# Feed-forward tiles of 512 tokens with matmuls of 512 columns, two output banks, and x @ w_in sharing its banks with y

## The chip, the cores and the metric

The kernel runs on one core of one Trainium2 chip. The metric is the device time of one launch in microseconds, as a median over several timed runs. A core has a matrix engine (TensorE; PE in the profile, with its weight loads listed apart as PEld), VectorE (DVE), ScalarE (ACT), GpSimd (POOL) and SyncE (SP), which issues the DMAs. Matmul results go to PSUM; in this kernel all of its eight banks (2 KB per partition, 512 fp32 columns) are handed out to named pools.

## The reference, cut to what matters

A chunked state-space scan over 4 batches, 8 heads and 768 positions makes a vector of 256 for each of 3072 tokens; a feed-forward layer with the nonlinearity h - tanh(h) follows.

```python
# x (4, 8, 768, 32), a (4, 8, 768), B and C (4, 8, 768, 16)
for c in range(nc):                       # chunks of the sequence
    cum = np.cumsum(la, axis=-1)          # la = log a of the chunk
    M = einsum('bhin,bhjn->bhij', Cc, Bc) * exp(cum_i - cum_j) * causal
    y[chunk] = M @ xc + (Cc @ state) * exp(cum)
    state = decay_full * state + sum_j(Bc_j xc_j * decay_from_j)
x = y.transpose(0, 2, 1, 3).reshape(3072, 256)
h = x @ w_in                              # (256, 2048)
out = (h - np.tanh(h)) @ w_out            # (2048, 256)
```

## The kernel before, in words

**Scan.** Each batch is cut into 7 chunks, six of Q = 112 positions and one of 96, 28 chunks in all. The 16 rows ahead of a chunk's positions hold the state, so that one matmul gives both the part within the chunk and the part from the state. For a chunk, `chunk_a` (lines 424 to 470) makes `att` on PE (lines 437 and 443), ACT takes the exponential (447), DVE multiplies (451), POOL masks (454), and the result `lt` is the moving operand of `chunk_y` (472 to 529): its matmuls (488) write `y` to a PSUM bank, eight heads times 112 positions, and those of line 496 write the new state beside it. ACT copies the state in four pieces into the next chunk's operand (`fn_c`, 501), ACT rounds y to `xh` (508), and DVE takes the rest as `xl` (513). `y` has one bank. From chunk 9 on the `att` of the next chunk is issued with the `y` of this one. Chunks 0 to 2 go through `first_tile`, which does not use `rt_c`. `rt_c` and `lt_c` hold the cumulative sums of the decays as bf16 parts; they come back from DRAM by DMAs in `get_parts` (780 to 785), and before that DVE fills `rt_c` (415).

**Feed-forward.** The 3072 tokens are 12 tiles of TT = 256, and the 2048 hidden columns are 8 pairs u of two blocks of 128. A step is one tile t and one pair u. `mm1` (532 to 551) makes `ph` = x @ w_in for the pair: two blocks times six matmuls of 256 columns (high by high, high by low, low by high, each over two halves of the 256 features), into one of the two banks of pool `ph`. `act` (553 to 582): ACT tanh (561), DVE h - tanh (565), ACT rounding to `gh` (569), DVE rest `gl` (576). `mm2` (584 to 613), LAG = 2 steps later in the written order, adds the pair to both halves of the output with twelve matmuls of 256 columns (602). Both halves e = 0, 1 stand side by side in the one bank of pool `po`. At the last tile the second half goes to a part of the `att` banks instead (named `end`). The result is copied to `ob` (640 to 644) and stored (647).

**Order.** Tiles 0 to 3 go through four passes of two pairs each, since the weights arrive and are split while they run (`conv`, 272 to 319, on ACT and DVE); their partial outputs are kept in `pt` (618, 625). Tiles 4 to 11 take all 8 pairs in one go. Chunks are planned into the steps of the tile ahead of the one that needs them. All operations are first recorded in `Order` (lines 48 to 187) with an engine, an estimated cost, and what they read and write. A buffer is a slot of a named ring; slots of a ring are taken in the order of recording, and a slot can be taken when the readers of its last user are done. `Order` then tries 16 list schedules and issues the instructions in the order of the shortest. Each engine runs its instructions in that order.

Of the kernel before, what the change touches and what calls it, by code (L numbers as in the profile page):

```python
# [30 lines left out]
TT = 256  # L31
NT = T // TT
# [158 lines left out]
def tile_ssm_moe(ctx: ExitStack, tc: tile.TileContext, a, x, bn, bc, wts, out):  # L191
# [9 lines left out]
    ps_y = ctx.enter_context(tc.tile_pool(name="ps_y", bufs=1, space=PSUM))  # L201
# [155 lines left out]
    def first_tile():  # L357
# [39 lines left out]
        for ck in range(len(chunks[0])):  # L397
# [74 lines left out]
    def chunk_y(ck):  # L472
# [31 lines left out]
        def fn_h():  # L504
            if c == 0:
                seq[b]["xh"] = p3.tile([P, 2, S], F32R, tag="xh", name=f"xh{b}", bufs=2)
            k["yv"] = k["y"][:, 0 : 2 * Q].rearrange("p (g q) -> p g q", g=2)[:, :, 0:q]
            nc.scalar.copy(seq[b]["xh"][:, :, c * Q : c * Q + q], k["yv"])

        def fn_l():  # L510
            if c == 0:
                seq[b]["xl"] = p3.tile([P, 2, S], F32R, tag="xl", name=f"xl{b}", bufs=2)
            nc.vector.tensor_tensor(out=seq[b]["xl"][:, :, c * Q : c * Q + q], in0=k["yv"],  # L513
                                    in1=seq[b]["xh"][:, :, c * Q : c * Q + q].bitcast(F32), op=ALU.subtract)
# [17 lines left out]
    def mm1(t, u):  # L532
        b, j = divmod(t, S // TT)
        d, ts = seq[b], slice(j * TT, (j + 1) * TT)
        cs = [c for c in range(CPB) if c * Q < ts.stop and (c + 1) * Q > ts.start]
        n_h, n_g = slot("ph", NPH), slot("g", 3)
        gs[t, u, 0] = [n_h, n_g]

        def fn():
            ph = ps_h.tile([P, 2, TT], F32, tag="ph", name=f"ph{t}_{u}")  # L540
            gs[t, u] = [ph]
            for j in range(2):

                for p in range(2):
                    for k in range(2):
                        for w_ in (wh, wl)[: 2 - p]:
                            nc.tensor.matmul(out=ph[:, j, :], lhsT=w_[:, u, 0, k, j * P : (j + 1) * P],  # L547
                                             rhs=d[("xh", "xl")[p]][:, k, ts], start=p == 0 and k == 0 and w_ is wh,
                                             stop=p == 1 and k == 1, skip_group_check=True)

        op("PE", 1.41, fn, r=[*[d["n_xh"][c] for c in cs], *[d["n_xl"][c] for c in cs], f"wh{u}.0", f"wl{u}.0"], w=[n_h])

    def act(t, u, eng):
        n_h, n_g = gs[t, u, 0]
        n_gh, n_gl = slot("gh", 3), slot("gl", 3)
        gs[t, u, 0] += [n_gh, n_gl]

        def fn_t():
            g = p3.tile([P, 2, TT], F32, tag="g", name=f"g{t}_{u}")
            gs[t, u].append(g)  # L560
            nc.scalar.activation(g, gs[t, u][0], AF.Tanh)  # L561

        def fn_s():
            ph, g = gs[t, u]
            nc.vector.tensor_tensor(out=g, in0=ph, in1=g, op=ALU.subtract)  # L565

        def fn_h():
            gh = p3.tile([P, 2, TT], F32R, tag="gh", name=f"gh{t}_{u}")
            nc.scalar.copy(gh, gs[t, u][1])  # L569
            gs[t, u].append(gh)  # L570

        def fn_l():
            _, g, gh = gs[t, u]
            gl = p3.tile([P, 2, TT], F32R, tag="gl", name=f"gl{t}_{u}")
            on = nc.vector if eng == "DVE" else nc.gpsimd
            on.tensor_tensor(out=gl, in0=g, in1=gh.bitcast(F32), op=ALU.subtract)  # L576
            gs[t, u].append(gl)
# [4 lines left out]
        op(eng, 0.8 if eng == "DVE" else 1.8, fn_l, r=[n_g, n_gh], w=[n_gl])  # L582

    def mm2(t, u, seg):

        _, _, n_h, n_l = gs[t, u, 0]
        if u == seg[0]:
            n_po[t, seg] = slot("po", 1)

        def fn():  # L590
            _, _, gh, gl = gs[t, u]
            if u == seg[0]:
                po[t, seg] = [ps_o.tile([P, 2, TT], F32, tag="po", name=f"o{t}_{u}")] * 2
                if end:

                    po[t, seg][1] = ps_a.tile([P, 2, TT], F32, tag="att", name="end")

            for es in ((0,), (1,)) if end and u == seg[-1] else ((0, 1),):
                for k, (w_, g) in enumerate(((wh, gh), (wl, gh), (wh, gl))):
                    for j in range(2):  # L600
                        for e in es:
                            nc.tensor.matmul(out=po[t, seg][e][:, e, :], lhsT=w_[:, u, 1, j, e * P : (e + 1) * P],  # L602
                                             rhs=g[:, j, :], start=u == seg[0] and k == 0 and j == 0 and (e == 0 or end),
                                             stop=u == seg[-1] and k == 2 and j == 1, skip_group_check=True)
# [10 lines left out]
    def keep(t, seg):  # L615

        if seg[0]:
            op("DVE", 0.69, lambda: nc.vector.tensor_tensor(out=pts[t], in0=po[t, seg][0], in1=pts[t], op=ALU.add),
               r=[n_po[t, seg]], w=[n_pt[t]])
            return  # L620
        n_pt[t] = slot("pt", NSW)

        def fn():
            pts[t] = p1.tile([P, 2, TT], F32, tag="pt", name=f"pt{t}", bufs=NSW)
            nc.scalar.copy(pts[t], po[t, seg][0])

        op("ACT", 0.6, fn, r=[n_po[t, seg]], w=[n_pt[t]])

    def store(t, seg):
        name = op.pieces(slot("ob", 2), 2)  # L630

        def fn_c(i):
            if i == 0:
                obs[t] = p2.tile([P, 2, TT], F32, tag="ob", name=f"ob{t}")
                if t == NT - 1:

                    obs["end"] = p2.tile([P, 2, TT], F32, tag="ob", name="ob_end")
            ob1 = obs["end" if t == NT - 1 else t][:, 1]
            if t in pts:
                nc.vector.tensor_tensor(out=obs[t], in0=po[t, seg][0], in1=pts[t], op=ALU.add)  # L640
            elif i == 0:
                nc.scalar.copy(obs[t][:, 0], po[t, seg][0][:, 0])
            else:
                nc.vector.tensor_copy(out=ob1, in_=po[t, seg][1][:, 1])

        def fn_d(i):
            nc.sync.dma_start(out=out[i * P : (i + 1) * P, t * TT : (t + 1) * TT], in_=obs["end" if t == NT - 1 and i else t][:, i])

        if t < NSW:
            op("DVE", 0.69, lambda: fn_c(0), r=[n_po[t, seg], n_pt[t]], w=name)  # L650
        else:
            op("ACT", 0.36, lambda: fn_c(0), r=[n_po[t, seg]], w=[name[0]])
            op("DVE", 0.36, lambda: fn_c(1), r=[n_po[t, seg]], w=[name[1]])
        for i in range(2):
            op("SP", 0.42, lambda i=i: fn_d(i), r=[name[i]], dma=KB)
# [23 lines left out]
    rt_c = cp.tile([P, 2, NCK, P], BF16, name="rt_c")  # L679
# [100 lines left out]
    def get_parts(i, k, sl):  # L780
        src = cum3[i // 2].rearrange("p (e w c) m -> p e w c m", e=2, w=2)[:, i % 2, :, sl].rearrange("p w c m -> p w (c m)")
        if k == 0:
            nc.sync.dma_start(out=lt_c[32 * i + 3 : 32 * i + 9, sl], in_=src)
        else:
            nc.sync.dma_start(out=rt_c[32 * i : 32 * i + 3, :, sl].rearrange("p w c m -> p w (c m)"), in_=src)

    n_pr = slot("y", 1)
# [7 lines left out]
    n_pq2 = slot("po", 1)  # L795
# [98 lines left out]
```

## Time and profile before

| what | value |
|---|---|
| timed runs | 345.36, 346.02, 348.71 us |
| median | 346.02 us |
| span of the profiled execution, first to last instruction | 342.5 us |
| median less that span | 3.5 us |
| busy: PE, PEld, DVE, ACT, POOL | 328.7, 318.0, 226.9, 193.3, 54.2 us |
| matmuls of 256 columns | 2304, at lines 547 and 602 |
| mean granted TensorE clock | 0.980 of full |

The profiled execution has no time of its own in the records beside its span; where a time is compared, the median stands for it. The page of the profile gives busy time and share per engine, 40 slices of the span as tenths of busy time with the granted clock, the chain of work that ended last followed back from the end, and groups of equal instructions with what they waited for. The trace can also be asked for the instructions in order of time, for busy times in chosen windows, and for all uses of one tile. A busy PE is not PE at its peak: matmuls overlap, so distances between starts are read instead of durations.

### The profile page before, as it was taken

Reading aid. Unit: us, or ns where it says so; the run is one execution under the profiler, and the core shown is the slowest. Engines: PE = TensorE matmul, PEld = TensorE weight load, DVE = VectorE, ACT = ScalarE, POOL = GpSimd, SP = SyncE. Lnnn points to the kernel's source line nnn. Section 1 sums busy time; section 2 is a strip of 40 time slices with the busy share of each in tenths; the row PEclk is TensorE's granted clock in tenths of the full one; section 3 lists DMA queues with packets and bytes.
Section 4 is the critical chain, followed back from the end, with each engine's and each line's share of the span. In section 5 each row is a group of like instructions: output and inputs, shape, how many; then the busy total and the mean of one; then the engine's idle time right before and its main releaser. Section 6 shows DMA issues by size and latency. Waiting matters only on the chain.

```text
span 342.5 us, 8855 instructions
## 1 busy us (share of the span) xinstructions
PE 328.7 (96%) x3756; PEld 318.0 (93%) x3756; DVE 226.9 (66%) x339; ACT 193.3 (56%) x403; POOL 54.2 (16%) x69
## 2 busy tenths in 40 slices
PE   9759879999999999999999999999999999999996
PEld 7648769999999999999999999999999999999996
DVE  5898999989899656744655654654655654654552
ACT  8866788857453445734745644634645654534441
POOL 1536444101000101210211210210211110100000
PEclk9956999999999999999999999999999999999999
DMA  5939693910000012300301210210200000000000
GB/s 173 272 90 286 165 297 103 257 45 15 16 2 0 2 59 80 92 15 2 91 15 31 63 31 2 63 29 2 63 3 1 33 2 2 31 2 2 31 2 32
DMA packets 12471, 21.39 MB, mean 62 GB/s; under 512 B 2848, under 2 KB 7648, under 8 KB 12432
## 3 DMA queue, kind: packets, MB, share of 16 engines
q1 hardware_dynamic: 12432, 20.84, 21.0%
q8 instruction: 29, 0.48, 0.6%
q14 instruction: 10, 0.08, 0.1%
HBM read 17.51 MB, written 3.32 MB: 61 GB/s over the span
## 4 chain that ended last, share of the span: by engine, by line
PE 91%; DVE 5%; ACT 1%; POOL 1%; issue 1%; POOLq 0%; DVEq 0%; ACTq 0%
PE ph L547 40%; PE o L602 38%; PE y L488 4%; PE att L443 3%; PE end L602 2%; PE att L437 1%; PE warm L729 1%; DVE lt L389 1%; DVE wm L295 1%; PE y L496 1%; DVE lt L451 1%; DVE rt_c L415 1%; PE cp L366 1%; DVE wv L299 1%; POOL lt L394 0%
## 5 line engine op out<-in xcount | busy, mean ns | idle before, releaser
L561 ACT ACTIVATE g<-ph 128x512 f32<-128x512 f32 x96 | 57.4, 598 | 82.3 <-PE ph L547 78.5
L565 DVE TENSOR_TENSOR g<-ph,g 128x512 f32<-128x512 f32 x96 | 66.1, 689 | 55.4 <-ACT g L561 54.5
L547 PE MATMUL ph<-xh,wh 128*128 128x256 f32 x384 | 101.4, 286 | 0.0
L547 PE MATMUL ph<-xh,wl 128*128 128x256 f32 x384 | 100.2, 282 | 0.0
L576 DVE TENSOR_TENSOR gl<-g,gh 128x512 fp32r<-128x512 f32 x96 | 67.9, 708 | 28.7 <-ACT gh L569 27.4
L569 ACT CAST gh<-g 128x512 fp32r<-128x512 f32 x96 | 59.3, 619 | 34.0 <-DVE g L565 32.9
L547 PE MATMUL ph<-xl,wh 128*128 128x256 f32 x384 | 77.0, 282 | 0.0
L547 PEld LDWEIGHTS ph<-xh,wh 128*128 128x128 f32 x384 | 73.2, 191 | 1.4 <-issue 0.4
L547 PEld LDWEIGHTS ph<-xh,wl 128*128 128x128 f32 x384 | 73.1, 190 | 0.0
L602 PE MATMUL o<-gh,wh 128*128 128x256 f32 x368 | 61.2, 284 | 0.0
L602 PE MATMUL o<-gh,wl 128*128 128x256 f32 x368 | 59.6, 279 | 0.0
L602 PE MATMUL o<-gl,wh 128*128 128x256 f32 x368 | 59.6, 279 | 0.0
L547 PEld LDWEIGHTS ph<-xl,wh 128*128 128x128 f32 x384 | 59.6, 190 | 0.0
L454 POOL TENSOR_SCALAR_AFFINE_SELECT lt<-lt 128x896 f32<-128x896 f32 (+1 forms) x25 | 28.2, 1128 | 155.5 <-DVE lt L451 150.9
L602 PEld LDWEIGHTS o<-gh,wh 128*128 128x128 f32 x368 | 50.5, 188 | 1.5
L602 PEld LDWEIGHTS o<-gl,wh 128*128 128x128 f32 x368 | 50.6, 188 | 0.0
L602 PEld LDWEIGHTS o<-gh,wl 128*128 128x128 f32 x368 | 50.5, 187 | 0.0
L451 DVE TENSOR_TENSOR lt<-att,lt 128x896 f32<-128x896 f32 (+1 forms) x25 | 26.7, 1067 | 11.3 <-ACT lt L447 11.1
L447 ACT ACTIVATE lt<-att 128x896 f32<-128x896 f32 (+1 forms) x25 | 22.6, 905 | 11.2 <-PE att L443 10.7
L501 ACT COPY x<-y 16x64 f32<-16x64 f32 x96 | 19.5, 203 | 7.6 <-DVE xl L513 6.9
L488 PE MATMUL y<-lt,x 128*32 128x112 f32 (+1 forms) x448 | 17.1, 272 | 7.0 <-POOL bc L337 3.0
L330 POOL TENSOR_TENSOR bw<-braw,wdec 128x256 f32<-128x256 f32 x14 | 13.2, 945 | 52.1 <-PE y L496 47.7
(77 smaller groups left out, 249.9 us busy)
## 6 DMA issues: line engine op xcount, KB each, us to landing
raw<-w_d SPq DMA_DIRECT2D x16, 512.0 KB
x<-x_d SPq DMA_DIRECT2D x14, 256.0 KB
bc<-bc_d SPq DMA_DIRECT2D x56, 60.0 KB
out_d<-ob SPq DMA_DIRECT2D x23, 128.0 KB
braw<-bn_d SPq DMA_DIRECT2D x14, 112.0 KB
cum<-parts SPq DMA_DIRECT2D x1, 168.0 KB
out_d<-ob_end SPq DMA_DIRECT2D x1, 128.0 KB
lt_c<-cum SPq DMA_DIRECT2D x4, 27.0 KB
```

The costliest lines, as they stand in the source:

```text
L330: nc.gpsimd.tensor_tensor(out=d["b"].rearrange("p c (h n) -> p c h n", h=H), in0=d["braw"].rearrange("p c (h n) -> p c h n", h=H), in1=wd. ...
L447: nc.scalar.activation(k["l"][:, :, 0:q].rearrange("p (i w) q -> p i w q", i=4), k["a"][:, :, 0:2, :], AF.Exp)
L451: nc.vector.tensor_tensor(out=lt, in0=k["a"][:, :, 2:4, :], in1=lt, op=ALU.mult)
L454: nc.gpsimd.affine_select(out=k["l"][:, :, 0:q], in_=k["l"][:, :, 0:q], pattern=[[0, H], [1, q]], compare_op=ALU.is_ge, fill=0.0, base=N, ...
L488: nc.tensor.matmul(out=y[D * h : D * h + D, hg * Q : hg * Q + q], lhsT=d["x"][:, cg, P * hg + D * h : P * hg + D * h + D], rhs=k["l"][:, 4 ...
L501: nc.scalar.copy(grp[(ck + 1) // CPG]["x"][0:N, (ck + 1) % CPG, 2 * D * i : 2 * D * i + 2 * D], k["y"][D * i : D * i + N, H * D : H * D + ...
L547: nc.tensor.matmul(out=ph[:, j, :], lhsT=w_[:, u, 0, k, j * P : (j + 1) * P], rhs=d[("xh", "xl")[p]][:, k, ts], start=p == 0 and k == 0 an ...
L561: nc.scalar.activation(g, gs[t, u][0], AF.Tanh)
L565: nc.vector.tensor_tensor(out=g, in0=ph, in1=g, op=ALU.subtract)
L569: nc.scalar.copy(gh, gs[t, u][1])
L576: on.tensor_tensor(out=gl, in0=g, in1=gh.bitcast(F32), op=ALU.subtract)
L602: nc.tensor.matmul(out=po[t, seg][e][:, e, :], lhsT=w_[:, u, 1, j, e * P : (e + 1) * P], rhs=g[:, j, :], start=u == seg[0] and k == 0 and ...
```

## The change

- Tiles 0 to 3 keep 256 tokens; tokens 1024 to 3071 are four tiles of 512 (`WIDTH`). A step of a wide tile is one block of 128 hidden columns in place of a pair: six matmuls of 512 columns in `mm1`, six in `mm2`. `ph`, `g`, `gh` and `gl` keep their size of 128x512.
- The output has two banks, `po0` and `po1`, one for each half. `mm2` goes through all matmuls of half 0 and then through those of half 1. Keeping and storing is done half by half, on 128x256 for narrow and 128x512 for wide tiles. The special case of the last tile is gone.
- Pool `y` is gone. The `y` of chunks 0 to 2 and the sums at the start use `po0` and `po1`; from chunk 3 on `y` takes a slot of the ring `ph`, which stays at two banks.
- `xh` and `xl` are one ring of 1536 positions in place of two buffers of 768, so that the tile of tokens 2048 to 2559 can lie across two batches.
- `rt_c` is 112 wide in place of 128; its loads become two DMAs in place of one, eight more in all. `parts` moves to the buffers of `ob`.
- Planner costs: 1.31 for a wide block of matmuls beside 1.41 for a narrow pair.

```diff
-TT = 256
-NT = T // TT
+WIDTH = 256, 256, 256, 256, 512, 512, 512, 512
+NT = len(WIDTH)
+START = [sum(WIDTH[:t]) for t in range(NT + 1)]
+BANK = 512
+RING = 2 * S
...
-    ps_y = ctx.enter_context(tc.tile_pool(name="ps_y", bufs=1, space=PSUM))
...
     def chunk_y(ck):
-        n_y = slot("y", 1)
+        at0 = b % 2 * S + c * Q
+        tag = f"po{1 - ck % 2}" if ck < len(chunks[0]) else "ph"
+        n_y = slot(tag, NPH if tag == "ph" else 1)
...
-            y = k["y"] = ps_y.tile([P, 2 * H * D], F32, tag="y", name=f"y{ck}")
+            y = k["y"] = (ps_h if tag == "ph" else ps_o).tile([P, BANK], F32, tag=tag, name=f"y{ck}")
...
-            nc.scalar.copy(seq[b]["xh"][:, :, c * Q : c * Q + q], k["yv"])
+            nc.scalar.copy(xh[:, :, at0 : at0 + q], k["yv"])
...
-    def mm1(t, u):
+    def blocks(t):
+        return BANK // WIDTH[t]
+
+    def mm1(t, f):
+        w = WIDTH[t]
+        ts = slice(START[t] % RING, START[t] % RING + w)
...
-            for j in range(2):
+            for i in range(blocks(t)):
+                u, j = divmod(f + i, 2)
                 for p in range(2):
                     for k in range(2):
                         for w_ in (wh, wl)[: 2 - p]:
-                            nc.tensor.matmul(out=ph[:, j, :], lhsT=w_[:, u, 0, k, j * P : (j + 1) * P],
-                                             rhs=d[("xh", "xl")[p]][:, k, ts], ...
+                            nc.tensor.matmul(out=ph[:, i * w : i * w + w], lhsT=w_[:, u, 0, k, j * P : (j + 1) * P],
+                                             rhs=(xh, xl)[p][:, k, ts], ...
-        op("PE", 1.41, fn, ...
+        op("PE", 1.41 if w == 256 else 1.31, fn, ...
...
     def mm2
-            n_po[t, seg] = slot("po", 1)
+            n_po[t, seg] = [slot(f"po{e}", 1) for e in range(2)]
...
-            for es in ((0,), (1,)) if end and u == seg[-1] else ((0, 1),):
+            for e in range(2):
                 for k, (w_, g) in enumerate(((wh, gh), (wl, gh), (wh, gl))):
-                    for j in range(2):
-                        for e in es:
-                            nc.tensor.matmul(out=po[t, seg][e][:, e, :], lhsT=w_[:, u, 1, j, e * P : (e + 1) * P],
-                                             rhs=g[:, j, :], ...
+                    for i in range(blocks(t)):
+                        u, j = divmod(f + i, 2)
+                        nc.tensor.matmul(out=po[t, seg][e][:, 0:w], lhsT=w_[:, u, 1, j, e * P : (e + 1) * P],
+                                         rhs=g[:, i * w : i * w + w], ...
...
     def store(t, seg):
+        for e in range(2):
+            old = [n_pt[t][e]] if t < NSW else []
+            op("DVE" if t < NSW or e else "ACT", cost, lambda e=e: fn_c(e), r=[n_po[t, seg][e], *old], w=[name[e]])
+            op("SP", 0.42, lambda e=e: fn_d(e), r=[name[e]], dma=KB * w // 256)
...
-    rt_c = cp.tile([P, 2, NCK, P], BF16, name="rt_c")
+    rt_c = cp.tile([P, 2, NCK, Q], BF16, name="rt_c")
...
     def get_parts(i, k, sl):
-            nc.sync.dma_start(out=rt_c[32 * i : 32 * i + 3, :, sl].rearrange("p w c m -> p w (c m)"), in_=src)
+            for w in range(2):
+                nc.sync.dma_start(out=rt_c[32 * i : 32 * i + 3, w, sl], in_=src[:, w, :, N:P])
...
-    segs = [(t, tuple(range(i, j))) for i, j in zip(SWEEPS, SWEEPS[1:]) for t in range(NSW)]
-    segs += [(t, tuple(range(NCONV))) for t in range(NSW, NT)]
+    segs = [(t, (2 * i, 2 * j)) for i, j in zip(SWEEPS, SWEEPS[1:]) for t in range(NSW)]
+    segs += [(t, (0, NF)) for t in range(NSW, NT)]
+    steps = [(t, f, seg) for t, seg in segs for f in range(*seg, blocks(t))]
```

More of the change, by code (lines that the diff above doesn't have):

```diff
@@ L210, in tile_ssm_moe @@
     for t in range(NT):
-        b, j = divmod(t, S // TT)
-        end = b * CPB + -(-(j + 1) * TT // Q)
+        b, r = divmod(START[t + 1] - 1, S)
+        end = b * CPB + r // Q + 1
         chunks[t], ends = list(range(ends, end)), end
@@ L436, in fn_p @@
                 r = slice(32 * i, 32 * i + 9)
-                nc.tensor.matmul(out=at_[:, i, 0:2, :], lhsT=lt_c[r, ck], rhs=rt_c[r, :, ck, N : N + q],
+                nc.tensor.matmul(out=at_[:, i, 0:2, :], lhsT=lt_c[r, ck], rhs=rt_c[r, :, ck, 0:q],
                                  start=True, stop=True)
@@ L529, in chunk_y @@
         op("DVE", 0.4, fn_l, r=[n_y, n_xh], w=[n_xl])
-    def mm1(t, u):
-        b, j = divmod(t, S // TT)
-        d, ts = seq[b], slice(j * TT, (j + 1) * TT)
-        cs = [c for c in range(CPB) if c * Q < ts.stop and (c + 1) * Q > ts.start]
+    def blocks(t):
[3 more added lines that the diff above has]
+        ts = slice(START[t] % RING, START[t] % RING + w)
+        n = [x for b in seq for c in range(CPB) if b * S + c * Q < START[t] + w
+             and b * S + min((c + 1) * Q, S) > START[t] for x in (seq[b][0][c], seq[b][1][c])]
         n_h, n_g = slot("ph", NPH), slot("g", 3)
-        gs[t, u, 0] = [n_h, n_g]
+        gs[t, f, 0] = [n_h, n_g]
         def fn():
-            ph = ps_h.tile([P, 2, TT], F32, tag="ph", name=f"ph{t}_{u}")
-            gs[t, u] = [ph]
-            for j in range(2):
+            ph = ps_h.tile([P, BANK], F32, tag="ph", name=f"ph{t}_{f}")
+            gs[t, f] = [ph]
+            for i in range(blocks(t)):
+                u, j = divmod(f + i, 2)
                 for p in range(2):
@@ L546, in fn @@
                         for w_ in (wh, wl)[: 2 - p]:
[L547 to L548 removed]
+                            nc.tensor.matmul(out=ph[:, i * w : i * w + w], lhsT=w_[:, u, 0, k, j * P : (j + 1) * P],
+                                             rhs=(xh, xl)[p][:, k, ts], start=p == 0 and k == 0 and w_ is wh,
@@ L569, in fn_h @@
-            nc.scalar.copy(gh, gs[t, u][1])
-            gs[t, u].append(gh)
+            gh = p3.tile([P, BANK], F32R, tag="gh", name=f"gh{t}_{f}")
+            nc.scalar.copy(gh, gs[t, f][1])
+            gs[t, f].append(gh)
         def fn_l():
[L573 to L577, printed above, removed]
+            _, g, gh = gs[t, f]
@@ L579, in act @@
+            gl = p3.tile([P, BANK], F32R, tag="gl", name=f"gl{t}_{f}")
+            nc.vector.tensor_tensor(out=gl, in0=g, in1=gh.bitcast(F32), op=ALU.subtract)
+            gs[t, f].append(gl)
         op("ACT", 0.6, fn_t, r=[n_h], w=[n_g])
@@ new lines, in act, with mm2 @@
+        op("DVE", 0.71, fn_l, r=[n_g, n_gh], w=[n_gl])
+    def mm2(t, f, seg):
+        w, last = WIDTH[t], f + blocks(t) == seg[1]
+        _, _, n_h, n_l = gs[t, f, 0]
+        if f == seg[0]:
+            n_po[t, seg] = [slot(f"po{e}", 1) for e in range(2)]
+        def fn():
+            _, _, gh, gl = gs[t, f]
+            if f == seg[0]:
+                po[t, seg] = [ps_o.tile([P, BANK], F32, tag=f"po{e}", name=f"o{t}_{f}_{e}") for e in range(2)]
+            for e in range(2):
+                for k, (w_, g) in enumerate(((wh, gh), (wl, gh), (wh, gl))):
+                    for i in range(blocks(t)):
+                        u, j = divmod(f + i, 2)
+                        nc.tensor.matmul(out=po[t, seg][e][:, 0:w], lhsT=w_[:, u, 1, j, e * P : (e + 1) * P],
+                                         rhs=g[:, i * w : i * w + w], start=f == seg[0] and k == 0 and i == 0,
+                                         stop=last and k == 2 and i == blocks(t) - 1, skip_group_check=True)
+        op("PE", 1.41 if w == 256 else 1.31, fn, r=[n_h, n_l, f"wh{f // 2}.1", f"wl{f // 2}.1"], w=n_po[t, seg])
+        if last:
+            if seg[1] < NF:
@@ L615, in keep @@
     def keep(t, seg):
[L617 to L627, printed above, removed]
+        w = WIDTH[t]
+        cost = 0.36 if w == 256 else 0.6
@@ new lines, in keep, with fn @@
+        if seg[0] == 0:
+            n_pt[t] = op.pieces(slot(f"pt{t}", 1), 2)
+        def fn(e):
+            o = po[t, seg][e][:, 0:w]
+            if seg[0]:
+                nc.vector.tensor_tensor(out=pts[t][:, e], in0=o, in1=pts[t][:, e], op=ALU.add)
+                return
+            if e == 0:
+                pts[t] = p1.tile([P, 2, w], F32, tag=f"pt{t}", name=f"pt{t}")
+            nc.scalar.copy(pts[t][:, e], o)
+        for e in range(2):
+            op("DVE" if seg[0] else "ACT", cost, lambda e=e: fn(e), r=[n_po[t, seg][e]], w=[n_pt[t][e]])
@@ L629, in store, with fn_c @@
     def store(t, seg):
+        w = WIDTH[t]
+        cost = 0.36 if w == 256 else 0.6
         name = op.pieces(slot("ob", 2), 2)
[L632 to L638, printed above, removed]
+        def fn_c(e):
+            if e == 0:
+                obs[t] = p2.tile([P, 2, w], F32, tag="ob", name=f"ob{t}")
+            o, out_ = po[t, seg][e][:, 0:w], obs[t][:, e]
@@ L639, in fn_c @@
             if t in pts:
-                nc.vector.tensor_tensor(out=obs[t], in0=po[t, seg][0], in1=pts[t], op=ALU.add)
-            elif i == 0:
-                nc.scalar.copy(obs[t][:, 0], po[t, seg][0][:, 0])
-            else:
[L644 to L653, printed above, removed]
@@ L654, in store, with fn_d @@
-        for i in range(2):
-            op("SP", 0.42, lambda i=i: fn_d(i), r=[name[i]], dma=KB)
+                nc.vector.tensor_tensor(out=out_, in0=o, in1=pts[t][:, e], op=ALU.add)
+            elif e == 0:
+                nc.scalar.copy(out_, o)
+            else:
+                nc.vector.tensor_copy(out=out_, in_=o)
+        def fn_d(e):
+            nc.sync.dma_start(out=out[e * P : (e + 1) * P, START[t] : START[t] + w], in_=obs[t][:, e])
+        for e in range(2):
+            old = [n_pt[t][e]] if t < NSW else []
+            op("DVE" if t < NSW or e else "ACT", cost, lambda e=e: fn_c(e), r=[n_po[t, seg][e], *old], w=[name[e]])
+            op("SP", 0.42, lambda e=e: fn_d(e), r=[name[e]], dma=KB * w // 256)
@@ L672, in tile_ssm_moe @@
     wdec = cp.tile([P, H, NCK], F32, name="wdec")
-    rows = p2.tile([P, 2, TT], F32, tag="ob", name="rows")[:, 0].rearrange("p (i q) -> p i q", i=2)
-    rest = p2.tile([P, 2, TT], F32, tag="ob", name="rest")[:, 0].rearrange("p (i q) -> p i q", i=2)
-    parts = cp.tile([P, 2, 3, P], BF16, name="parts")
+    both = p2.tile([P, 2, 2, P], F32, tag="ob", name="both")
+    rows, rest = both[:, 0], both[:, 1]
+    xh = cp.tile([P, 2, RING], F32R, name="xh")
+    xl = cp.tile([P, 2, RING], F32R, name="xl")
+    parts = p2.tile([P, 2, 3, P], BF16, tag="ob", name="parts")
     lt_c = cp.tile([P, NCK, P], BF16, name="lt_c")
-    rt_c = cp.tile([P, 2, NCK, P], BF16, name="rt_c")
+    rt_c = cp.tile([P, 2, NCK, Q], BF16, name="rt_c")
     cum3 = dr.tile([2, 3, 4 * NCK, P], BF16, name="cum3")
@@ L753, in sums_rows @@
     def sums_rows():
-        pr = misc["pr"] = ps_y.tile([P, 4, P], F32, tag="y", name="pr")
+        pr = misc["pr"] = ps_o.tile([P, 4, P], F32, tag="po1", name="pr")
         misc["pq"] = pr.rearrange("p i q -> p (i q)")[:, 2 * P :]
@@ L838, in tile_ssm_moe @@
         if g < len(steps):
-            t, u, _ = steps[g]
-            mm1(t, u)
-            act(t, u, "DVE")
+            t, f, _ = steps[g]
+            mm1(t, f)
+            act(t, f)
             for fn, args in todo.get(g, ()):
```

62 lines of the change are left out of this document (20 added, 42 removed).

## The prediction

> **What bounds the kernel now.** I read the page first: shares, slices, chain.
>
> ```profile
> span 342.5 us, 8855 instructions
> PE 328.7 (96%) x3756; PEld 318.0 (93%) x3756; DVE 226.9 (66%) x339; ACT 193.3 (56%) x403; POOL 54.2 (16%) x69
> PE   9759879999999999999999999999999999999996
> PEclk9956999999999999999999999999999999999999
> PE 91%; DVE 5%; ACT 1%; POOL 1%; issue 1%; POOLq 0%; DVEq 0%; ACTq 0%
> ```
>
> PE is the chain, and PE is full from the eighth slice on. Then the busy times by stage:
>
> ```profile
> 20.00:40.00 20.00, 16.38 (x248) 14.84 (x252) 18.16 (x24) 12.74 (x30) 9.10 (x10) 0.69 0.73 210
> 40.00:60.00 20.00, 18.08 (x308) 16.80 (x309) 19.51 (x26) 16.58 (x40) 9.09 (x9) 1.00 0.66 189
> 60.00:80.00 20.00, 20.00 (x172) 20.00 (x171) 18.68 (x25) 13.78 (x22) 2.23 (x3) 1.00 0.44 128
> ...
> 160.00:180.00 20.00, 20.00 (x262) 19.28 (x265) 12.02 (x17) 11.24 (x26) 2.85 (x4) 1.00 0.16 46
> ...
> 300.00:320.00 20.00, 20.00 (x172) 20.00 (x172) 9.70 (x16) 8.25 (x16) 0.00 (x0) 1.00 0.01 1
> ```
>
> The columns are the stretch, its length, PE, PEld, DVE, ACT and POOL busy (with counts), the granted clock, DMA share, GB/s. Before 60 us DVE is nearly full and PE has gaps; from 60 us PE has none, with DVE and ACT near half load after 160. So there the time is the number of matmuls times the distance between their starts (the pitch). That pitch and what moves it:
>
> ```profile
> 192.57 2.83 PE ph L547 x24
> ...
> 24.00:27.00 3.00, 3.00 (x16) 2.71 (x13) 3.00 (x5) 2.26 (x4) 1.12 (x1) 0.50 0.65 161
> 24.45 0.41 PE L547 MATMUL ph<-xh,wl 128*128 128x256 f32 x1
> 26.37 0.63 PE L547 MATMUL ph<-xl,wh 128*128 128x256 f32 x2
> ...
> 5.27 0.54 PE L763 MATMUL pr<-la,upto 128*128 128x224 f32 x2
> 5.65 1.94 PE L366 MATMUL cp<-upto,la 128*128 128x112 f32 x16
> 7.51 0.71 PE L377 MATMUL att<-bc 16*128 16x112 f32 x16
> 5.27:5.65 0.38, 0.38 (x5) 0.38 (x4) 0.00 (x0) 0.37 (x3) 0.24 (x1) 1.00 0.91 334
> 5.65:7.51 1.86, 1.86 (x17) 1.75 (x16) 1.56 (x5) 1.86 (x2) 0.00 (x0) 1.00 1.06 371
> ```
>
> The chain's row gives 2.83 / 24 = 117.9 ns for 256 columns at full clock. At clock 0.50 nine matmuls lie between 24.45 and 26.37: 213.3 ns, so 106.7 for the columns alone at full clock. Some 11 ns are thus not columns. What they are, the start of the kernel tells, at clock 1.00: sixteen cp matmuls of 112 columns take 5.65 to 7.51, 116.3 ns each; two pr matmuls of twice the columns, also fp32 with 128x128 weights, take 190 ns each. If fp32 costs two cycles a column, 224 columns are 186.7 ns and 112 are 93.3. The long one pays 3.3 ns over its columns, the short one is held at 116. So about 117 ns looks like a floor for one matmul that brings 128x128 weights, whatever its columns, and above it little is added.
>
> **The change part by part.** *512 columns.* Of 2304 feed-forward matmuls (the rows L547 and L602 of the page: 3 x 384, 3 x 368, and 3 x 16 into "end") tiles 4 to 11 hold 1536; they become 768 of 512 columns, with half the weight loads. Pitch of a new one: at least 213.3 (columns alone); at most 235.8 (two old ones, nothing gained); 224.5 if 11.2 ns go with every matmul. I take 213.3 + 3.3 = 216.6, by the pr row, the nearest stream longer than the floor. Gain 768 x (235.8 - 216.6) = **14.7 us** (17.3 at 213.3; 8.7 at 224.5; 0).
>
> The Trainium skill, "TensorE: Matmul & The Clock Gate", section "Back-to-back issue gap", gives the isolated gap as N/2.4 + 2.5 ns. For 512 that is 215.8 and the gain would be 15.4 us; for 256 it gives 109.2, where the trace has 117.9. The same page's section on LDWEIGHTS has 128 columns loading in 106.7 ns: the floor read above is 10 ns over it.
>
> *y takes a bank of ph.* I call m(g) the twelve (or six) matmuls that make step g's ph, and m2 those that take its g to the output. From chunk 3 on y is one more user of the two ph banks, in the written order m, y, m. The block m(g+1) behind y needs the bank of m(g), and m(g+2) needs y's.
>
> ```profile
> 312.32 0.63 PE L602 MATMUL o<-gh,wh 128*128 128x256 f32 x4
> 312.58 0.60 ACT L561 ACTIVATE g<-ph 128x512 f32<-128x512 f32 x1 [0.85 <-PE ph L547]
> 313.21 0.69 DVE L565 TENSOR_TENSOR g<-ph,g 128x512 f32<-128x512 f32 x1 [0.76 <-ACT g L561]
> ...
> 161.09 0.59 PE L488 MATMUL y<-lt,x 128*32 128x112 f32 x16
> 162.38 0.39 PE L547 MATMUL ph<-xh,wh 128*128 128x256 f32 x1
> 163.40 0.34 ACT L508 CAST xh<-y 128x224 fp32r<-128x224 f32 x1
> 165.01 0.39 DVE L513 TENSOR_TENSOR xl<-y,xh 128x224 fp32r<-128x224 f32 x1 [0.38 <-ACT x L501]
> 165.44 0.42 ACT L501 COPY x<-y 16x64 f32<-16x64 f32 x2 [0.46 <-DVE xl L513]
> ```
>
> An m frees its bank 313.90 - 312.32 = 1.6 us after PE leaves it. Between two m with a y between lie an m2 (6 x 216.6 = 1.3 us) and y with its att (162.38 - 161.09 = 1.3): 2.6, enough. The bank of y is read by four state copies (0.2 each), the xh cast (0.34) and the xl subtract (0.39): 1.5 us of work, about 2.1 with hand-overs; in the trace it was held 161.09 to 165.86, 4.8 us, with an exp and a tanh between, when nobody waited for it. Under the change PE lays att, m(g+1), m2 over it: from the start of y 1.3 + 1.3 + 1.3 = 3.9 us, and 5.2 with a second m2. So a hold as lazy as now stalls PE by up to 0.9 us, one by priority not at all; behind the waiting m stand further m2 and the next y. Eighteen chunks fall after 60 us: 0 to 16 us; I take **+1.0**, since ACT and DVE are half idle there and the planner counts these bank dependences.
>
> *Before 60 us.* The ring now fixes an order: y5 behind m3, y7 behind m5.
>
> ```profile
> 39.92 0.59 PE L488 MATMUL y<-lt,x 128*32 128x112 f32 x16
> 40.63 3.04 PE ph L547 x24
> 43.75 0.54 PE L488 MATMUL y<-lt,x 128*32 128x96 f32 x16
> 46.80 0.59 PE L488 MATMUL y<-lt,x 128*32 128x112 f32 x16 [1.83 <-DVE xl L513]
> 57.84 2.83 PE ph L547 x24
> ...
> L785 SPq DMA_DIRECT2D rt_c<-cum x8: 273/430/443, 16.5 to 39.9; - x8
> ```
>
> Today y5 (39.92) runs ahead of m2 and m3 (40.63), y7 (46.80) ahead of m4. Behind them each loses the two m, some 2.8 us, and the state is serial, so y9 and the dense stretch from 57.84 slip by up to 5 us; against that m5 and its m2 are done earlier (2.8 us off the dense part), and the 1.83 us wait for the single y bank can go. Eight more rt_c loads cost SP 8 x 0.43 = 3.4 us of issue, half of it ahead of the loads that follow the first four of them. The narrower rt_c gives DVE an eighth of its four rt_c instructions back, which I count at nothing. Bounds -1.8 to +5; I take **+1.5**.
>
> *Two output banks.* Keeping and storing the 256-wide tiles makes two 128x256 instructions of one 128x512, some 2 x 0.42 - 0.69 = 0.15 us more of ACT or DVE each time (rows of the end, below); PE runs full over it, and the first bank is ready half a block sooner. The gl operand is needed four matmuls earlier (4 x 117.9 = 0.47 us), covered by the two steps that lie between a block's m and its m2. Cost 0; were that cover gone, 16 passes at 0.15 us and 0.47 at each late gl. The ring for x removes no work: 0.
>
> *The end.*
>
> ```profile
> 339.38 0.42 DVE L644 COPY ob_end<-end 128x256 f32<-128x256 f32 x1 [2.84 <-PE end L602]
> 339.83 0.33 SPq L647 DMA_DIRECT2D out_d<-ob_end  x1
> ...
> L565 DVE TENSOR_TENSOR g<-ph,g 128x512 f32<-128x512 f32 x96 | 66.1, 689 | 55.4 <-ACT g L561 54.5
> ```
>
> The last copy becomes 128x512, which DVE reads from PSUM in 0.69: +0.27. The last store doubles to 256 KB: 0 to +1; **+0.7** in all.
>
> Sum: 342.5 - 14.7 + 1.0 + 1.5 + 0.7 = 331.0 of span. The runs lie around 346.02, 3.5 above the span: **334.5**.
>
> **The rivals.**
> A, *a fixed price per matmul*: 11.2 ns also at 512. For it: that is the plainest reading of 117.9 against 106.7. Against: the pr row pays 3.3. 342.5 - 8.7 + 3.2 + 3.5 = 340.5.
> B, *y blocks the ring* (ends slower): y holds its bank as long as today and arrives late, so each m(g+2) waits. Place: after each of 18 y. It eats the gain from (14.7 - 2.2) / 18 = 0.7 us each, a hold of 4.6 us from y's start; with 1.3 us (a hold of 5.2) the time is 342.5 - 14.7 + 23.4 + 2.2 + 3.5 = 356.9. For it: today's 4.8. Against: half-idle engines.
> C, *nothing from width*: the pitch is a rate per column, 235.8. Half clock cannot refute this (it would hide there too); the cp and pr rows do, if fp32 behaves as I read it. 342.5 + 3.2 + 3.5 = 349.2.
> D, *the clock falls*: many short waits between the wide blocks take the clock to half as in 18 to 27 us.
>
> ```profile
> 18.14 0.59 PE L488 MATMUL y<-lt,x 128*32 128x112 f32 x16 [2.09 <-DVE lt L389]
> 18.00:22.00 4.00, 0.91 (x39) 0.85 (x43) 3.97 (x7) 2.71 (x8) 3.25 (x4) 0.60 0.05 13
> 44.00:46.80 2.80, 0.97 (x36) 0.68 (x25) 2.69 (x5) 2.80 (x6) 2.16 (x2) 1.00 0.93 315
> ```
>
> It fell with PE at 0.91 of 4.0 us, and held with 0.97 of 2.8; so only stalls above B's would do it. If a third of the wide stretch (128 blocks at 1.3 is 166 us) ran at half clock, that would add 55: 390.
> The same page of the Trainium skill ("A second HAM failure mode: psum-queue depth-cycling") tells of such an oscillation at 512 columns with banks cycled; no row here shows it.
> E, *more than a column per cycle*: wide matmuls overlap until only the floor of 117.9 counts, 768 x (216.6 - 117.9) = 75.8 us more, 258.7. The half-clock row, at exactly a column per cycle, speaks against it. The Trainium skill, same page, "Back-to-back issue gap", states about 131 ns sustained for 512; by that the gain would be 768 x (235.8 - 131) = 80 us.
>
> **How the numbers follow.** Forecast 0.73, with its own range 328 to 339 (pitch 213.3 to 219, waits 0 to 5); A 0.11, B 0.09, C 0.04, D 0.02, E 0.01. The range 328 to 343 takes in the forecast, A and the mild end of B, 0.84 in all, less what lies at the edges. About 1% (3.5 us) is what a measurement can tell here. Faster: the forecast, A (0.10), E and a third of B: 0.87 less 0.02 for edges, 0.85. Same: C, and a ninth of B and of A each: 0.06. Slower: the rest of B, D, and mishaps before 60 us: 0.09.
>
> **What would show it.** In the chain of the new profile six wide matmuls make a block of 1.30 us (A: 1.35; C: 1.41). PE stays at 20.00 of 20 in every window after 62 us; the waits list would name xl or the state copies ahead of ph for B. The dense stretch begins near 59 instead of 57.84. The last DVE copy takes 0.69. The forecast is wrong if the pitch is above 220 or PE waits after 62 us add to over 5 us.

## The result, and the profile after

The changed kernel takes 347.7 us (median of 347.54 to 348.54) against 345.7 for the kernel before measured beside it: 1.010 of it, 95% interval 1.006 to 1.0145. The ratios in this text, with their intervals, come from the undisturbed executions of both kernels alone, so they are not quotients of the medians. I had forecast 334.5. The page of the changed kernel first: span, busy times, the slices of PE and of the granted clock.

```profile
span 346.0 us, 7399 instructions
PE 327.3 (95%) x2988; PEld 280.8 (81%) x2988; DVE 229.0 (66%) x347; ACT 195.0 (56%) x403; POOL 52.2 (15%) x69
PE   9857989699999999999999999999999999999995
PEclk9978989989999999999999999999999999999999
```

768 matmuls fewer, PEld 37 us less, and PE busy only 1.4 us less. To find the place I cut both traces at the 385th matmul into `ph`, the first of tile 4 and in the changed kernel the first wide one; by then all m of tiles 0 to 3 are issued. The windows of the matmuls into `ph` show it by their counts (384 matmuls ahead of the cut, 768 narrow or 384 wide behind; the columns are PE and PEld on that tile, clock, DMA share, GB/s). First the kernel before, then the changed one:

```profile
0.00:132.74 132.74, 51.36 (x384) 48.90 (x385) 0.95 0.41 118
132.74:339.34 206.60, 100.21 (x768) 94.25 (x768) 1.00 0.09 26
```

```profile
0.00:143.01 143.01, 54.46 (x384) 51.31 (x385) 0.95 0.39 114
143.01:341.95 198.94, 96.86 (x384) 71.87 (x384) 1.00 0.07 22
```

The cut comes 10.3 us later. By then the changed kernel has done 14 chunks' y and 15 att where the other had done 12 and 13; at 1.3 us for each pair that is 2.6 us of work done early, so 7.7 us are lost ahead of the cut. Behind it the stretch is 7.7 us shorter, of which the same 2.6 are chunk work that is no longer there: 5.1 us won by width, not 14.7. From the last matmul to the end of the span it is 346.02 - 341.95 = 4.1 in place of 342.49 - 339.34 = 3.15. 10.3 - 7.7 + 0.9 is the 3.5 us by which the spans differ.

The two prices in the trace of the changed kernel. First the pitch, in a row of the chain of work that ended last:

```profile
300.75 2.75 PE ph L550 x12
```

The worst wait, on PE in order of time (start, duration, instruction, and in brackets the wait ahead of it):

```profile
61.75 0.38 PE L550 MATMUL ph<-xh,wh 128*128 128x256 f32 x1 [0.46 <-ACT xh L509]
...
67.96 0.59 PE L491 MATMUL y<-lt,x 128*32 128x112 f32 x16 [2.54 <-issue]
68.34 0.33 PE L499 MATMUL y<-x,bw 128*16 128x32 f32 x16
68.60 0.28 PE L439 MATMUL att<-rt_c,lt_c 9*128 9x224 bf16 x4
68.70 0.62 PE L445 MATMUL att<-bc 16*128 16x112 f32 x16
69.25 0.58 PE L550 MATMUL ph<-xh,wh 128*128 128x256 f32 x1
```

I write y10 for the y of chunk 10, and so on. What y10 waits for the trace does not name ("issue"). But y10 takes the bank that m6 had, two places ahead of it in a ring of two, and the last to read that bank is DVE, in h - tanh(h). From the same trace, m6's last matmuls, then the ACT and DVE instructions that bear on it:

```profile
63.61 0.40 PE L550 MATMUL ph<-xl,wh 128*128 128x256 f32 x2
64.29 1.07 ACT L305 CAST wh<-wv 128x1024 fp32r<-128x1024 f32 x1
65.24 1.10 ACT L564 ACTIVATE g<-ph 128x512 f32<-128x512 f32 x2
65.78 1.47 DVE L294 TENSOR_SCALAR wv<-wv 128x1024 f32<-128x1024 f32 x1
67.18 1.27 DVE L568 TENSOR_TENSOR g<-ph,g 128x512 f32<-128x512 f32 x2
```

The first of the two subtractions takes 0.68 us and ends at 67.86, 0.1 us before y10 starts; POOL had masked y10's operand by 66.71. So the bank of m6 came free 3.9 us after its last matmul ended (64.0), with the splitting of weights (the `wh` and `wv` rows) running ahead of its two readers on ACT and DVE. In e3_b_yring and e6_own_to_9 below the subtraction of m6 ends just as close ahead of y10 (65.38 and 65.48; 70.03 and 70.14). That is read from the traces; freeing the bank sooner was not tried.

And the clock, in three windows of all engines (PE, PEld, DVE, ACT, POOL, then clock, DMA share, GB/s):

```profile
21.50:28.20 6.70, 4.98 (x34) 4.54 (x35) 5.31 (x7) 3.29 (x8) 0.95 (x4) 0.50 0.48 120
48.80:52.10 3.30, 3.30 (x18) 3.30 (x17) 3.30 (x5) 0.60 (x1) 2.16 (x2) 0.50 0.99 314
69.30:72.60 3.30, 3.30 (x19) 3.30 (x16) 2.92 (x5) 2.06 (x7) 0.00 (x0) 0.50 0.58 186
```

Twelve wide matmuls take 2.75 us, 228.9 ns each (2.747 by the unrounded starts). And where the kernel before was dense from 57.84 on, this one still waits at 65 to 68 us, ahead of y10; its m8 starts 7.5 us after m6 (69.25 against 61.75; 62.08 against 57.84 before). From 1.3 us after the wait's end the granted clock is 0.50 for some 3.4 us, in which PE is busy throughout; the window at 49 us, behind a shorter wait, is like it. The first window, at 21.5 us, is the counterpart of a longer one in the kernel before (shown further below).

### The profile page after: what moved, and what is told of

It reads as the page before. It is cut to its first block, busy times and chain, and to the rows that moved or that the text cites. A ratio compares the mean times of both kernels' runs of the same rounds, so it can differ in the third digit from the quotient of the medians.

```text
span 346.0 us, 7399 instructions
## 1 busy us (share of the span) xinstructions
PE 327.3 (95%) x2988; PEld 280.8 (81%) x2988; DVE 229.0 (66%) x347; ACT 195.0 (56%) x403; POOL 52.2 (15%) x69
## 4 chain that ended last, share of the span: by engine, by line
PE 83%; DMA 6%; DVE 3%; SPq 2%; issue 2%; ACT 2%; POOL 1%
PE ph L550 38%; PE o L601 38%; PE y L491 3%; PE att L445 3%; DMA x<-x_d 2%; DMA bc<-bc_d 2%; DMA braw<-bn_d 2%; PE att L439 1%; DVE lt L453 1%; POOL lt L456 1%; ACT lt L449 1%; SPq L234 1%; PE y L499 1%; DVE wl L308 1%; SPq L786 1%
## 5 line engine op out<-in xcount | busy, mean ns | idle before, releaser
L550 PE MATMUL ph<-xh,wh 128*128 128x256 f32 (+1 forms) x256 | 86.1, 346 | 0.5 <-ACT xh L509 0.5
L550 PE MATMUL ph<-xh,wl 128*128 128x256 f32 (+1 forms) x256 | 85.5, 344 | 0.0
L601 PE MATMUL o<-gh,wh 128*128 128x256 f32 (+1 forms) x256 | 77.8, 345 | 0.0
L601 PE MATMUL o<-gl,wh 128*128 128x256 f32 (+1 forms) x256 | 75.7, 336 | 0.6 <-DVE gl L578 0.6
L601 PE MATMUL o<-gh,wl 128*128 128x256 f32 (+1 forms) x256 | 75.8, 337 | 0.0
L550 PE MATMUL ph<-xl,wh 128*128 128x256 f32 (+1 forms) x256 | 66.9, 343 | 1.3 <-DVE xl L512 1.3
L550 PEld LDWEIGHTS ph<-xh,wh 128*128 128x128 f32 x256 | 50.1, 196 | 6.5 <-ACT xh L509 0.8
L550 PEld LDWEIGHTS ph<-xh,wl 128*128 128x128 f32 x256 | 50.2, 196 | 5.3
L550 PEld LDWEIGHTS ph<-xl,wh 128*128 128x128 f32 x256 | 45.3, 196 | 6.9 <-DVE xl L512 1.7
L491 PEld LDWEIGHTS y<-lt,x 128*32 128x32 f32 x448 | 10.4, 109 | 13.2 <-issue 7.9
```

The source lines that it names most:

```text
L491: nc.tensor.matmul(out=y[D * h : D * h + D, hg * Q : hg * Q + q], lhsT=d["x"][:, cg, P * hg + D * h : P * hg + D * h + D], rhs=k["l"][:, 4 ...
L550: nc.tensor.matmul(out=ph[:, i * w : i * w + w], lhsT=w_[:, u, 0, k, j * P : (j + 1) * P], rhs=(xh, xl)[p][:, k, ts], start=p == 0 and k = ...
L601: nc.tensor.matmul(out=po[t, seg][e][:, 0:w], lhsT=w_[:, u, 1, j, e * P : (e + 1) * P], rhs=g[:, i * w : i * w + w], start=f == seg[0] and ...
```

## The experiments

Theory R: the order that y is forced into, as a member of the ring ph, costs the time ahead of the cut. Theory S: the eight more rt_c loads on the SP queue cost it. For the pitch (fp32r is the type of the rounded operands `xh`, `wh` and `gh`): a rate per fp32r column, other engines at work beside it, or a price of the weights.

**Columns, types and weights (e1_probe).** Added behind the changed kernel's last work, 24 matmuls of each form:

```diff
+    for m in probe(1, 512, P, wr, xr[:, 0:512]):   # fp32r, 128x128 weights; 384 and 256 likewise
+        nc.tensor.matmul(**m)
+    for m in probe(4, 512, P, wb, xb[:, 0:512]):   # bf16, 128x128 weights; 256 likewise
+        nc.tensor.matmul(**m)
+    for m in probe(6, 512, 32, wn, xr[:, 0:512]):  # fp32r, 128x32 weights; 256 likewise
+        nc.tensor.matmul(**m)
```

> The changed kernel with seven rows of 24 matmuls added behind its last work, when ACT and DVE are idle: fp32r operands at 512, 384 and 256 columns and bf16 operands at 512 and 256 columns, all with 128x128 weights, then fp32r at 512 and 256 columns with 128x32 weights. The kernel's own wide blocks have a pitch of 228.9 ns and its narrow ones 117.9. Theory 1, a rate per fp32r column: the idle rows repeat 229 at 512 and give about 174 at 384, while bf16 falls to about 216 at 512, and narrower weights change nothing at 512. Theory 2, ACT and DVE slow the stream: the idle fp32r row at 512 falls to about 216. Theory 3, a fixed price for each change of weights: 32-column weights bring fp32r at 512 to about 216, and bf16 stays near 229.

The seven rows on PE in order of time; a pitch is the distance from one row's start to the next row's, by 24, or, where said so, the mean distance of the starts within a row:

```profile
338.29 5.66 PE L858 MATMUL probe<-xh,wh 128*128 128x512 f32 x24
343.78 4.32 PE L860 MATMUL probe<-xh,wh 128*128 128x384 f32 x24
347.94 2.98 PE L862 MATMUL probe<-xh,wh 128*128 128x256 f32 x24
350.76 5.35 PE L864 MATMUL probe<-rt_c,lt_c 128*128 128x512 bf16 x23
355.95 2.78 PE L866 MATMUL probe<-rt_c,lt_c 128*128 128x256 bf16 x24
358.49 5.80 PE L868 MATMUL probe<-xh,wh 128*32 128x512 f32 x24
364.13 2.89 PE L870 MATMUL probe<-xh,wh 128*32 128x256 f32 x24
```

fp32r at 512, 384 and 256 columns: 228.8, 173.3 and 117.8 ns within the rows. That is a straight line, 55.5 ns for 128 columns (0.433 a column) and 7 ns beside it. bf16 at 512: 5.19 / 24 = 216.3 (one record is missing in that row, its place is not), and 109.2 within the row at 256. ACT and DVE are idle here and the wide blocks' 228.9 is repeated, so they do not slow it. With 32-column weights the 512-column row has not become faster. Its 5.64 / 24 = 235 holds one long distance, from its first matmul to its second (358.49 to 358.81); behind that it is 231.3:

```profile
358.81 5.49 PE L868 MATMUL probe<-xh,wh 128*32 128x512 f32 x23
```

(364.13 - 358.81) / 23 = 231.3. The 256-column row has become slightly faster (113.5 within the row). So the pitch is a rate of the fp32r stream, 4% over bf16's, plus a few ns; a wide matmul saves 2 x 117.9 - 228.9 = 6.9 ns against two narrow ones, 5.3 us over 768. That is the 5.1 of the windows.

**A bank of its own for y while the narrow tiles run (e2_hybrid, e5_hybrid).** One kernel, run twice; the profile below is of the second run.

```diff
-        tag = f"po{1 - ck % 2}" if ck < len(chunks[0]) else "ph"
+        tag = "po1" if ck < chunks[NSW][-1] + 1 else "ph"
...
-            n_po[t, seg] = [slot(f"po{e}", 1) for e in range(2)]
+            n_po[t, seg] = [slot("po0", 1)] * 2 if w == 256 else [slot(f"po{e}", 1) for e in range(2)]
```

> The changed kernel, but while tiles 0 to 3 run, y has a bank of its own again (chunks 0 to 13 in po1) and both halves of a narrow tile's output share po0; from chunk 14 on y is in the ring ph, and the wide tiles have their two output banks. Theory R (the forced order of y in the ring ph costs the time before the dense stretch): the first matmul of tile 4, at 143.0 us in the changed kernel, comes 5 to 8 us earlier, the span falls from 346.0 to 338 to 341, and the kernel beats the one before by 1 to 2%. Theory S (the eight more rt_c loads on the SP queue cost it): they are still there, so the span stays within 2 us of 346.

> The same kernel as e2_hybrid, for a profile at full clock and a narrower interval. Theory R: the first wide matmul starts 5 to 8 us ahead of 143.0 us; from there to the last matmul it takes the 199 us of the changed kernel, 5 us less than the kernel before for the same work; 0.98 to 0.99 of the kernel before.

340.9 us, 0.987 of the kernel before, interval 0.981 to 0.993 (0.988, 0.982 to 0.995, the first time). Windows of the matmuls into `ph` cut at the first wide block (PE, PEld, DVE and ACT on that tile, then clock, DMA share and GB/s, in this and the next kernels):

```profile
0.00:137.30 137.30, 54.00 (x384) 50.85 (x385) 21.62 (x32) 19.04 (x32) 0.94 0.41 119
137.30:336.24 198.94, 96.88 (x384) 71.92 (x384) 44.42 (x65) 38.29 (x64) 1.00 0.07 22
```

On PE in order of time, m6, y10 and m8:

```profile
60.37 0.28 PE L550 MATMUL ph<-xh,wh 128*128 128x256 f32 x1
...
63.28 0.59 PE L491 MATMUL y<-lt,x 128*32 128x112 f32 x16
...
64.69 0.39 PE L550 MATMUL ph<-xh,wh 128*128 128x256 f32 x1
```

The cut comes 5.7 us earlier than in the changed kernel, and the wide stretch has the same 198.94. Nothing was changed but the banks of y and of the narrow output (the second by itself is e8_one_po below), so theory R holds and S does not: the rt_c loads are still there. y10 again stands ahead of m8, but in a bank of its own it need not wait for that of m6: it runs at 63.28, while DVE reads m6's bank from 63.96 to 64.64, and m8 follows at 64.69. The clock is not what was won: PE is busy at half clock for 14.7 us here (windows 20.4 to 33.9 and 47.7 to 51.0), for 11.6 in the three windows of the changed kernel.

**The ring alone (e3_b_yring).** The kernel before, with y from chunk 3 on in the ring ph.

```diff
-        n_y = slot("y", 1)
+        tag = "y" if ck < len(chunks[0]) else "ph"
+        n_y = slot(tag, NPH if tag == "ph" else 1)
```

> The kernel before with one change: from chunk 3 on y takes a slot of the ring ph; the bank of y serves only the start. Theory R: the dense stretch begins 5 to 8 us later, and the time rises by about that, 1.5 to 2.3%. Theory S: no change beyond 0.5%.

1.011 of the kernel before, interval 1.007 to 1.016. Windows at the same cut:

```profile
0.00:137.33 137.33, 50.79 (x384) 48.41 (x385) 21.90 (x32) 19.13 (x32) 0.98 0.40 114
137.33:343.93 206.60, 99.13 (x768) 94.16 (x768) 44.25 (x64) 38.28 (x64) 1.00 0.09 26
```

4.6 us later at the cut than the kernel before, with the same work done, and exactly its 206.60 behind. That is a little under the 5 to 8 us expected, and the 1.1% under the 1.5 to 2.3. This trace has less time at half clock, PE busy for 5.7 us of it (21.8 to 28.5) against 9.97 before. Counting half of such time as lost, an estimate, that hides some 2 us of the ring's price. The ring costs ahead of the cut only; the sixteen y in it behind the cut cost nothing.

**The rt_c loads alone (e4_b_split).** The kernel before, with two loads for one.

```diff
-            nc.sync.dma_start(out=rt_c[32 * i : 32 * i + 3, :, sl]..., in_=src)
+            for w in range(2):
+                nc.sync.dma_start(out=rt_c[32 * i : 32 * i + 3, w, sl, N:P], in_=src[:, w]...[:, :, N:P])
```

> The kernel before with one change: each rt_c load is two DMAs of 112-wide rows in place of one of 128-wide rows, eight DMAs more in all. Theory S: 3 to 7 us slower. Theory R: within 1 us of the kernel before.

1.0017, interval 0.998 to 1.006. The loads are there (the tile's row: 16 in place of 8, 0.32 us each), and the time is that of the kernel before.

```profile
L786 SPq DMA_DIRECT2D rt_c<-cum x16: 234/318/454, 16.1 to 42.5; - x16
```

**Two output banks (e8_one_po).** The changed kernel with the second edit of e2_hybrid and without the first.

> The changed kernel with both halves of a narrow tile's output in po0, as before the change; y in the ring ph from chunk 3 on, as in the changed kernel. If the two output banks cost nothing, as the prediction had it, the time is that of the changed kernel, 347 to 348.5. If they are part of the loss, it is 1 us or more faster.

347.2 us, 1.0076 of the kernel before (1.004 to 1.011), and 1.010 (1.006 to 1.0145) with the two banks: no difference that can be told.

**Which y (e6_own_to_9, e7_own_to_9_late, e9_late).** y10 belongs to tokens that are needed at step 32, but it is planned at step 7. In the kernel before it ran at 81.8 us (its row on PE in order of time); in the ring it has to be issued between m7 and m8.

```profile
81.80 0.59 PE L488 MATMUL y<-lt,x 128*32 128x112 f32 x16
```


```diff
-        tag = "po1" if ck < chunks[NSW][-1] + 1 else "ph"     # e5_hybrid
+        tag = "po1" if ck < JOINT else "ph"                   # e6 and e7; JOINT is 10
...
         g0, n = begin["t", t - 1], begin["t", t] - begin["t", t - 1]
+        if t == NSW:
+            g0, n = g0 + 4, n - 4                             # e7; in e9, on the changed kernel, 8
```

> As e5_hybrid, but y has its own bank for chunks 0 to 9 only; from chunk 10 on, still in the narrow passes, it is in the ring ph. If the ring costs its time by ordering y5 and y7 behind m3 and m5 (the prediction's place), this is as fast as e5_hybrid. If it costs it where y10, planned at step 7 though its tokens are needed only at step 32, has to come ahead of the narrow m8, it is as slow as the changed kernel, 346 to 348.

> As e6_own_to_9, but chunks 10 to 13 are planned four steps later, so that y10 stands in the ring four m blocks later. If y10's early place is the cost, at least half of the difference between e6_own_to_9 and e5_hybrid comes back, 2 to 4 us. If the ring costs through the number of y in it, nothing comes back.

> The changed kernel with one line added: chunks 10 to 13 are planned from eight steps later, so that y10 no longer stands in the ring ph ahead of the narrow m8; everything else, the ring too, is as in the changed kernel. If y10's place is what makes PE wait 2.5 us before it and lose the clock behind it, the loss between the starts of m6 and m8 (7.5 us there, 4.2 in the kernel before) goes, the first wide matmul comes 3 to 6 us ahead of 143.0, and the time is 342 to 345. If it is the number of y in the ring, the wait moves to another y and the time stays within 1 us of 347.7.

In e7 and e9 the edit moves all four chunks 10 to 13 later, with their att, exp and mask, not y10 alone. e6: 350.9 us, 1.016 (1.010 to 1.022). e7: 342.9, 0.995 (0.993 to 0.997). e9: 345.0, 1.0007 (0.997 to 1.004), where the changed kernel had 1.010 (1.006 to 1.0145). Windows at the cut of e6, e7 and e9:

```profile
0.00:146.68 146.68, 54.56 (x384) 50.92 (x385) 21.76 (x32) 19.12 (x32) 0.91 0.38 111
```

```profile
0.00:137.93 137.93, 53.02 (x384) 50.16 (x385) 21.98 (x32) 19.15 (x32) 0.93 0.42 118
```

```profile
0.00:141.67 141.67, 51.19 (x384) 48.82 (x385) 21.64 (x32) 19.11 (x32) 0.94 0.40 115
```

m6 and m8 of e9 on PE, in order of time:

```profile
63.59 0.28 PE L550 MATMUL ph<-xh,wh 128*128 128x256 f32 x1
...
67.44 0.38 PE L550 MATMUL ph<-xh,wh 128*128 128x256 f32 x1 [0.86 <-DVE g L568]
```

In e9 m8 starts 3.8 us after m6 (67.44 against 63.6) in place of 7.5: planning chunks 10 to 13 later shrinks the wait there to 0.9 us, and takes 2.7 us of the time (345.0 against 347.7). No half clock follows it there, but the trace has more of it earlier (PE busy for 15.7 us of it, between 15.2 and 39.0). How much of the gain is y10's place in the ring, and how much the work of its chunk on ACT and DVE, e9 cannot tell. It also fell short of what I expected: the cut comes only 1.3 us earlier in its trace (141.67 against 143.01, 3 to 6 expected), and 345.0 is the upper end of the forecast 342 to 345. The other 4 us up to e5_hybrid (340.9) lie in the rest of the ring: e7, with y3 to y9 out of it and y10 to y13 in it but late, stands half-way at 342.9. m6, y10 and m8 of e6 on PE, then m6 and m8 of e7:

```profile
64.63 0.28 PE L550 MATMUL ph<-xh,wh 128*128 128x256 f32 x1
...
70.14 0.84 PE L491 MATMUL y<-lt,x 128*32 128x112 f32 x16 [2.63 <-POOL bw L332]
72.28 0.58 PE L550 MATMUL ph<-xh,wh 128*128 128x256 f32 x1
```

```profile
59.23 0.41 PE L550 MATMUL ph<-xh,wh 128*128 128x256 f32 x1
...
64.32 0.28 PE L550 MATMUL ph<-xh,wh 128*128 128x256 f32 x1
```

e6 does not add up: with y3 to y9 in a bank of their own it should lie at or under the changed kernel. m6 to m8 takes it 7.7 us, about as long as the changed kernel, behind the same wait of y10; but m6 itself starts only at 64.6 (59.2 in e7). By an estimate the clock accounts for the excess: PE is busy at half clock for 23.4 us in e6 (19.2 to 32.7, 39.7 to 46.4 and 70.4 to 77.1) against 11.6 in the changed kernel. Half of the difference, 5.9 us, is more than the 3.7 us by which the cut of e6 is later (146.68 against 143.01). Why its clock fell more often, and what else of the 5 us ahead of m6 is the order of its schedule, is open. From e6 to e7 8 us come back, more than the 2 to 4 expected, and a part of that is clock too (15.7 us of busy PE at half clock in e7).

## Why the prediction was wrong, point by point

- *The bound.* Right: PE has no idle from 80 us on in any of these kernels, and time behind the cut is counts times pitch.
- *The pitch of 216.6.* The step that failed, and the larger part of the miss: of the 14.7 us of gain 9.4 did not come. I read the two fp32 rows at the start as a floor of 117 ns plus 3.3 ns over the columns, and carried the 3.3 to fp32r. The probe shows another law for fp32r: 0.433 ns a column and 7 ns beside it, where the half-clock row gives 213.3 / 2 / 256 = 0.417 a column; 32-column weights take only 4 ns off at 256 columns. The fp32 rows do not show that limit (190 ns for 224 columns is 0.848 a column), nor does fp32r at half clock (213.3 ns, less than twice 117.8). With widths of 256 alone, the trace could not tell a price per column from one per matmul; I had both as A and C, and at 228.9 the truth lies between these, 4.4 above A and 6.9 below C. The Trainium skill, "TensorE: Matmul & The Clock Gate", section "Back-to-back issue gap", has N/2.4 + 2.5 ns: 215.8 and 109.2. bf16 agrees (216.3 and 109.2), fp32r does not (228.8 and 117.8). Its 131 ns for 512 in a sustained stream is shown by neither.
- *Before 60 us: +1.5, at most +5, and the ring behind 60 us: +1.0, rival B up to 16.* The second step that failed: ahead of the cut 7.7 are lost, where I had 2.5 for both. That y in the ring has to keep its place among the m was right, but I followed only y5 and y7 and stopped at y9. The step that broke is that an m frees its bank 1.6 us after PE leaves it, read at 312 us, where ACT and DVE are half idle. At 64 us they still split weights, the bank of m6 is held for 3.9 us, and y10 and with it m8 wait, although tile 4 comes 24 steps later. That is rival B's late y, in one place of its eighteen. Behind the cut the ring costs 0: 206.60 with y in the ring (e3_b_yring) or not, and in the wide kernels, which all have y in it there, PE shows no wait. m2 and att cover the hold, as worked out for a hold by priority.
- *The clock.* I put no price on it. It is at half for some 3.4 us at 49 and at 69 us, when PE has work: about 1.7 us each. Both stand behind waits; that the waits bring them about was not tried. The first follows a wait of only 0.99 us that ended at 48.32, so rival D's reading that only long stalls would lower the clock does not hold. But the early stretch is shorter in exchange. In the kernel before, the one stretch at half clock lay partly over waits (window with the columns as above, PE busy 9.97 of 13.50); the three of the changed kernel have 4.98 + 3.30 + 3.30 = 11.58, so that the clock's share of the 7.7 us is some 0.8 us, by half of the difference, and the waits have the rest:

```profile
18.90:32.40 13.50, 9.97 (x112) 9.08 (x116) 11.91 (x16) 7.38 (x19) 7.17 (x7) 0.50 0.67 189
```

- *SP's eight loads, two output banks.* 0 (e4_b_split), where the bounds had 3.4 us of issue on SP; and 0 (e8_one_po), as taken.
- *The end: +0.7.* 0.9, by these rows: the copy is 0.69 as expected.

```profile
341.91 1.13 SPq L648 DMA_DIRECT2D out_d<-ob  x2
341.99 0.69 DVE L645 COPY ob<-o 128x512 f32<-128x512 f32 x1 [3.01 <-PE o L601]
```

- *The sum.* With the measured terms, 342.5 - 5.1 + 7.7 + 0.9 = 346.0, the span. The offset to the time, 3.5, was also too large: this execution took 347.72, 1.7 above its span.

The wide tiles themselves are worth having: with y out of the ring while the narrow tiles run, they make the kernel faster than both, 340.9 us.

## What to carry to other kernels

Before counting on wider matmuls, measure the pitch at the new width, in the same type and at full clock: a distance between starts at one width does not tell what is paid per matmul from what is paid per column, and a row in another type may not have the same limit. When a buffer joins a ring whose slots are taken in a written order, list every member with the step at which it is planned and the step at which it is needed; one planned long ahead of its use, harmless in a ring of its own, now waits until its predecessor's bank is read, and holds up all that is written behind it. Take the time to free a bank from the stage where it is needed, not from a calmer one. Give such a member its place late, or its own slot until the crowded stage is over.

## What the hardware showed that I had not expected

- At full clock fp32r streams 4% slower than twice its own rate at half clock: 0.433 ns a column (228.8, 173.3, 117.8 ns at 512, 384, 256) against 0.417 (213.3 ns at 256, halved); bf16 0.418 (216.3, 109.2).
- Narrower weights did not help at 512 columns, but did at 256: with 128x32 weights 231.3 ns against 228.8 with 128x128, both fp32r at 512 columns; 113.5 against 117.8 at 256. Why is open.
- In the traces of before and after a few blocks of narrow matmuls ran at about 113 ns in place of 117.9 (below, two rows of the kernel before on PE in order of time: eight matmuls from 53.41 to 54.32, 113.8 by these starts), and I found nothing in the trace to set them apart.

```profile
53.41 0.62 PE L602 MATMUL o<-gh,wh 128*128 128x256 f32 x4
...
54.32 0.62 PE L602 MATMUL o<-gl,wh 128*128 128x256 f32 x4
```
